# Another hand-made order for the first group of the last layer of an attention, soft-MoE and Mish kernel

## The chip, the cores and the metric

The kernel runs on one core of a Trainium2 chip. The metric is device time in microseconds of one execution. Engines are called as in the profile: PE (TensorE, matmuls; PEld its weight loads), DVE (VectorE), ACT (ScalarE), POOL (GpSimd), SP (SyncE, which issues the DMAs here).

## The reference

Three layers in float32. Attention with rotary embedding over 4 x 8 heads of 576 x 64 gives x with 2304 tokens of 512. A soft mixture of 8 experts with 4 slots each replaces x by `c @ slot_out`, where c is the softmax over the 32 slots of a token. The last layer is the one at issue:

```
def _moe2_ref(x, w_in, w_out):
    h = x @ w_in                                    # 512 -> 2048
    sp = np.where(h > 20.0, h, np.log1p(np.exp(np.minimum(h, 20.0))))
    g = h * np.tanh(sp)                             # Mish
    return (g @ w_out)                              # 2048 -> 512
```

w_in and w_out come as float64 arrays: their words are turned into float32 on the chip.

## The kernel before

Since x is c (2304 x 32) times slot_out (32 x 512), the last layer first multiplies slot_out by w_in, and each token needs only a product over 32 slots. To keep float32 accuracy with the fast fp32r matmuls, operands are split into a rounded part and a difference ("h" and "l": wo_h and wo_l for w_out, gh and gl for g; ct and wst hold both parts in their rows).

The layer's work is cut into units (i, j): 256 tokens (i, nine blocks) by 256 of the 2048 inner columns (j, eight). Three blocks make a group: group 0 is units 0 to 23, j in the outer and i in the inner loop, so three units in a row share a j. I call these three a round. Per unit:

- `mish(u)` (L992): hp = wst x ct on PE (two matmuls, L997), Mish on ACT into gg (L1004), a rounded copy gh (L1006), and gl = gg - gh on DVE (L1009).
- `second(u)` (L1014): twelve matmuls of 512 columns into the output tiles o_ps (L1028). In group 0 the eight with gh come first, then the four with gl.

Ahead of each round in group 0, `inner_a(j)` makes m_wp = slot_out x w_in on PE (L974) and copies it on ACT (L975); `inner_b(j)` makes m_w on PE (L980), copies it to wst on ACT (L982) and takes the difference of its lower half on DVE (L983). The units of round j read that part of wst. m_wp, m_w and hp share two PSUM buffers.

w_out has 16 chunks of 128 rows. The first four were converted during attention; `parts_of(c)` loads one from scratch memory and splits it (wo_h on ACT, L939; wo_l on DVE, L940). The other twelve come raw (`load_out`, four buffers, L863) and are converted by `cv(c, k)`: "S" scales the two words on ACT (L871, L872), 1 to 5 are DVE steps (L874, L876, L879, L881, L883), "H" is wo_h on ACT (L885), "L" is wo_l on DVE (L887). `convert(n)` issues the next n DVE steps of the list that `stream()` yields. `second` of round j reads chunks 2j and 2j + 1.

The order is by hand: `pin` keeps each engine's instructions in program order, and every engine works its queue in that order. In the loop at the end, unit u does `mish(u)` (from unit 3 on with `convert(4)` between gh and gl), then `inner_a(j + 1)` with i = 0 or `inner_b(j + 1)` with i = 1, then the `second` of earlier units; the lag between `mish` and `second` grows from one unit to LOOK = 4 in the course of group 0:

```
        while done < u + 1 - min(LOOK, 1 + u // 4):
            second(done)
            done += 1
```

`warm(pool, tag, n)` (L553) issues n matmuls of 128 x 128 on constants whose result nobody reads; each is two passes on PE. `fetch((3, fb, 0))` loads a quarter of the converted w_in from scratch (scr_in, 1 MB).

Of the kernel before, what the change touches and what calls it, by code (L numbers as in the profile page):

```python
# [42 lines left out]
def kernel(  # L43
# [13 lines left out]
    nc = tc.nc  # L57
    NB, H, S, D = q.shape
# [44 lines left out]
    NFC = F2 // 128  # L103

    NCE = 4
# [16 lines left out]
    def fetch(key, behind=False):  # L122
        m, e, hf = key
        t = parts[key][0]
        if m == 3:
            lds = [(t.rearrange("p (c f) -> p c f", c=KDM), scr_in[e])]
        else:
            w = (w1, w2)[m - 1]
            n = w.shape[1] // 2
            lds = [(t.rearrange("p (c f) -> p c f", c=n // 128),  # L130
                    w[e, hf * n:(hf + 1) * n, :].rearrange("(c p) f -> p c f", p=128))]
            if (m, e // 4, hf) == (2, E // 4 - 1, 1):

                final.append(lds.pop())
                if len(final) == 4:
                    lds = [(o[:, c], i[:, c]) for c in range(n // 128) for o, i in final]
        for out, in_ in lds:
            ld = nc.sync.dma_start(out=out, in_=in_)
            if behind:
                tc.keep_in_program_order(ld)  # L140
# [44 lines left out]
    behind = []  # L185
# [363 lines left out]
    def warm(pool, tag, n):  # L549

        ps = pool.tile([128, 128], F32, tag=tag, name="warm")
        for _ in range(n):
            tc.keep_in_program_order(nc.tensor.matmul(ps, lhsT=ident, rhs=ident, start=True, stop=True))  # L553
# [269 lines left out]
    for eg in range(2):  # L823
        for hf in range(2):
            end = eg == 1 and hf == 1
            for fh, cc in [(fh, cc) for fh in range(2) for cc in range(2)]:
                c = 2 * hf + cc
# [30 lines left out]
    pin = tc.keep_in_program_order  # L858

    def load_out(c):  # L860

        if c < NFC:
            pin(nc.sync.dma_start(out=raws[c % 4], in_=w_out[c * 128:(c + 1) * 128, :].bitcast(U32)))  # L863

    def cv(c, k):

        lo, hi = words(raws[c % 4])
        w = ws3[c % 3]
        wb, sf = w.bitcast(U32), sg.bitcast(F32)
        if k == "S":  # L870
            pin(nc.scalar.activation(out=hi.bitcast(F32), in_=hi.bitcast(F32), func=AF.Copy, scale=2.0 ** -112))  # L871
            pin(nc.scalar.activation(out=lo.bitcast(F32), in_=lo, func=AF.Copy, scale=2.0 ** -52))  # L872
        elif k == 1:
            pin(nc.vector.tensor_scalar(out=sg, in0=hi, scalar1=0x80000000, scalar2=None, op0=ALU.bitwise_and))  # L874
        elif k == 2:
            pin(nc.vector.scalar_tensor_tensor(out=wb, in0=hi, scalar=3, in1=sg, op0=ALU.logical_shift_left,  # L876
                                               op1=ALU.bitwise_or))
        elif k == 3:
            pin(nc.vector.tensor_scalar(out=sg, in0=wb, scalar1=0xFF800000, scalar2=None, op0=ALU.bitwise_and))  # L879
        elif k == 4:  # L880
            pin(nc.vector.tensor_tensor(out=sf, in0=sf, in1=lo.bitcast(F32), op=ALU.mult))  # L881
        elif k == 5:
            pin(nc.vector.tensor_tensor(out=w, in0=w, in1=sf, op=ALU.add))  # L883
        elif k == "H":
            pin(nc.scalar.copy(wo_h[c], w))  # L885
        else:
            pin(nc.vector.tensor_tensor(out=wo_l[c], in0=w, in1=wo_h[c].bitcast(F32), op=ALU.subtract))  # L887

    so_ps = ps_m.tile([128, DM], F32, tag="m", name="so_ps")
    for eg in range(2):  # L890
        for hf in range(2):
            for cc in range(4):
                c = 4 * hf + cc
# [31 lines left out]
        take(*rooms.pop(0))  # L925
    ot = room(F32)
    obs = [ot[:, i * DM:(i + 1) * DM] for i in range(4)]
    for c in range(NCE):
        if c == 2:
            fetch((3, 0, 0), behind=True)  # L930
        pin(nc.sync.dma_start(out=wo_l[c].bitcast(F32), in_=scr_out[c]))
    for c in range(NCE, NCE + 4):
        load_out(c)
    fetch((3, 1, 0), behind=True)

    def parts_of(c):

        x = wo_l[c].bitcast(F32)
        pin(nc.scalar.copy(wo_h[c], x))  # L939
        pin(nc.vector.tensor_tensor(out=wo_l[c], in0=x, in1=wo_h[c].bitcast(F32), op=ALU.subtract))  # L940

    def stream():

        for c in range(NCE, NFC):
            yield c, 1
            yield c, 2
            if c > NCE:
                yield c - 1, "L"
            yield c, 3
            if c + 1 < NFC:  # L950
                yield c + 1, "S"
            yield c, 4
            load_out(c + 4)
            yield c, 5
            yield c, "H"
        yield NFC - 1, "L"

    steps2 = stream()
# [1 line left out]
    def convert(n):  # L960
        while n:
            x = next(steps2, None)
            if x is None:
                return
            cv(*x)
            n -= x[1] not in ("S", "H")

    def inner_a(j):

        fb, o = divmod(j * 256, 512)  # L970
        wi = parts[3, fb, 0][0].rearrange("p (c f) -> p c f", c=KDM)[:, :, o:o + 256]
        ps = ps_p.tile([128, 256], F32, tag="p", name="m_wp")
        for c in range(KDM):
            pin(nc.tensor.matmul(ps[32 * c:32 * c + 32, :], lhsT=s_t[:, c, :], rhs=wi[:, c, :], start=True, stop=True))  # L974
        pin(nc.scalar.copy(wps[j % 2], ps))  # L975

    def inner_b(j):

        ps = ps_p.tile([128, 256], F32, tag="p", name="m_w")
        pin(nc.tensor.matmul(ps, lhsT=rr, rhs=wps[j % 2], start=True, stop=True))  # L980
        dst = wst[:, j * 256:(j + 1) * 256]
        pin(nc.scalar.copy(dst, ps))  # L982
        pin(nc.vector.tensor_tensor(out=dst[64:128], in0=ps[64:128], in1=dst[64:128].bitcast(F32), op=ALU.subtract))  # L983
# [3 lines left out]
    NG = NFC // 2  # L987
    GR = 3
# [3 lines left out]
    def mish(u):  # L992
        i, j = units[u]
        hp = ps_p.tile([128, 2, 256], F32, tag="p", name="hp")
        for x in range(2):
            f = 2 * j + x
            pin(nc.tensor.matmul(hp[:, x, :], lhsT=wst[:, f * 128:(f + 1) * 128],  # L997
                                 rhs=ct[:, i * 256:(i + 1) * 256],
                                 start=True, stop=True))
        hp = hp.rearrange("p a n -> p (a n)")  # L1000
        gg = ggs[u % 3]
        gh = p6.tile([128, 512], F32R, tag="gh", name="gh", bufs=LOOK + 1)
        gl = p6.tile([128, 512], F32R, tag="gl", name="gl", bufs=LOOK + 1)
        pin(nc.scalar.activation(out=gg, in_=hp, func=AF.Mish))  # L1004

        pin((nc.scalar.copy if u < NG * GR else nc.vector.tensor_copy)(gh, gg))  # L1006
        if 2 < u < NG * GR:
            convert(4)
        pin(nc.vector.tensor_tensor(out=gl, in0=gg, in1=gh.bitcast(F32), op=ALU.subtract))  # L1009
        gs[u] = gh, gl  # L1010

# [2 lines left out]
    def second(u):  # L1014
        i, j = units[u]
        gh, gl = gs.pop(u)
        todo = [(n, x, k) for n in range(2) for x in range(2) for k in range(3)]
        if u < NG * GR:

            todo.sort(key=lambda y: y[2] == 2)  # L1020
        if j == 0:
            for n in range(2):
                ops[i, n] = ps_o.tile([128, DM], F32, tag="o", name="o_ps")
        for at, (n, x, k) in enumerate(todo):
            g_, w_ = ((gh, wo_h), (gh, wo_l), (gl, wo_h))[k]
            f = 2 * j + x
            cols = slice(x * 256 + n * 128, x * 256 + n * 128 + 128)
            pin(nc.tensor.matmul(ops[i, n], lhsT=g_[:, cols], rhs=w_[f], start=(j == 0 and (x, k) == (0, 0)),  # L1028
                                 stop=(j == NG - 1 and all(y[0] != n for y in todo[at + 1:]))))
            if j == NG - 1 and all(y[0] != n for y in todo[at + 1:]):  # L1030
                ob = obs[(2 * i + n) % 4]
                pin((nc.scalar.copy if n else nc.vector.tensor_copy)(ob, ops.pop((i, n))))  # L1032
                store(2 * i + n, ob)
# [14 lines left out]
            pos += n  # L1048

    LOOK = 4  # L1050
    inner_a(0)
    parts_of(0)
    inner_b(0)
    parts_of(1)
    done = 0
    for u in range(len(units)):
        g, j = units[u][0] // GR, units[u][1]
        i = units[u][0] % GR
        if g == 0 and i == 2 and j in (0, 2):
            fetch((3, 2 + j // 2, 0), behind=True)  # L1060
        mish(u)
        if u in (1, 2):
            parts_of(u + 1)
        if u == 2:
            cv(NCE, "S")
        if g == 0 and j + 1 < NG:
            if i == 0:
                inner_a(j + 1)
            elif i == 1:
                inner_b(j + 1)  # L1070

        while done < u + 1 - min(LOOK, 1 + u // 4):
            second(done)
            done += 1
    while done < len(units):
        second(done)
        done += 1
    ring.close()


# [48 lines left out]
```

## Time and profile before

| | us |
|---|---|
| median of 3 runs | 679.82 |
| lowest, highest | 678.02, 682.76 |
| the profiled execution | 678.98 |
| its span, first to last instruction | 677.2 |

Times in rows are microseconds from the start of the span. A timeline row gives start, duration, engine, line, operation, written tile <- read tiles, shape and count, and in brackets the engine's idle time before it and what ended that. Matmuls are pipelined: their durations overlap, and what one costs is read from the distance of the starts. Rows name many small buffers "room".

### The profile page before, as it was taken

How to read it: one execution, taken by the hardware profiler on the slowest of the kernel's cores; microseconds unless marked ns; L12 is line 12 of the kernel's file. 1: busy time of each engine (PE TensorE's matmuls, PEld its weight loads, DVE VectorE, ACT ScalarE, POOL GpSimd, SP SyncE). 2: the span in 40 equal slices, each digit the busy share in tenths (PEclk: the TensorE clock that was granted, in tenths of full speed). 3: DMA queues.
4: the chain of work that ended last, by engine and by line, in shares of the span. 5: the costliest groups of instructions: out<-in, count | busy, mean ns of one | idle time of the engine just before them, and what ended most of it. 6: DMA issues, size and time to landing. Idle time of an engine off the chain costs nothing. (4 is left out here: it accounts for less than half of the span.)

```text
span 677.2 us, 11071 instructions
## 1 busy us (share of the span) xinstructions
PE 625.3 (92%) x4006; PEld 461.1 (68%) x4006; DVE 410.7 (61%) x823; ACT 336.3 (50%) x758; POOL 217.1 (32%) x263
## 2 busy tenths in 40 slices
PE   1588999987999999999999998998999999999997
PEld 1565677665677667667677663366688888888885
DVE  6787888886687866656565433159994433343331
ACT  2566776684676656755665412168763221221221
POOL 5658868754967545425300010000000000000000
PEclk9899999999999999999999999989999999999999
DMA  9678699877786975346559479954300300030004
GB/s 263 159 193 230 177 273 267 226 212 227 195 246 211 289 187 136 99 112 185 125 172 312 179 260 367 382 212 155 121 6 0 94 1 0 1 94 0 1 0 94
DMA packets 59607, 109.43 MB, mean 162 GB/s; under 512 B 12832, under 2 KB 25248, under 8 KB 59040
## 3 DMA queue, kind: packets, MB, share of 16 engines
q1 hardware_dynamic: 59552, 108.72, 53.8%
q8 instruction: 32, 0.52, 0.3%
q14 instruction: 23, 0.19, 0.1%
HBM read 70.25 MB, written 9.96 MB: 118 GB/s over the span
## 5 line engine op out<-in xcount | busy, mean ns | idle before, releaser
L361 DVE TENSOR_REDUCE nmax<-s 128x1 f32<-128x576 f32 x144 | 108.0, 753 | 61.0 <-PE s L335 38.3
L367 ACT ACTIVATE P<-s,nmax 128x576 f32<-128x576 f32 x144 | 107.3, 745 | 41.0 <-DVE nmax L361 29.0
L1028 PE MATMUL o_ps<-wo_h,gh 128*128 128x512 f32 x288 | 115.4, 401 | 0.0
L1028 PE MATMUL o_ps<-wo_l,gh 128*128 128x512 f32 x288 | 113.5, 394 | 0.0
L1004 ACT ACTIVATE room<-hp 128x512 f32<-128x512 f32 x72 | 43.1, 598 | 117.4 <-PE hp L997 113.0
L1028 PE MATMUL o_ps<-wo_h,gl 128*128 128x512 f32 x288 | 100.4, 389 | 0.0
L333 PE MATMUL s<-qk_st 128*128 128x288 f32 x256 | 84.9, 346 | 11.9 <-ACT P L367 6.5
L374 PE MATMUL t<-cs,P 128*128 128x128 f32 x512 | 78.6, 281 | 4.8 <-ACT P L367 2.7
L410 ACT COPY PT<-t 128x512 f32<-128x512 f32 x92 | 53.6, 587 | 48.4 <-PE t L374 47.5
L429 PE MATMUL m_av<-PT,w 128*64 128x320 f32 (+1 forms) x384 | 73.3, 421 | 3.6 <-DVE PT L413 2.1
L374 PEld LDWEIGHTS t<-cs,P 128*128 128x128 f32 x512 | 59.3, 142 | 22.1 <-issue 10.9
L335 PE MATMUL s<-k_st,qk_st 128*128 128x288 f32 x256 | 73.0, 299 | 0.0
L333 PEld LDWEIGHTS s<-qk_st 128*128 128x128 f32 x256 | 49.2, 192 | 31.7 <-ACT P L367 10.7
L1006 DVE CAST gh<-room 128x512 fp32r<-128x512 f32 x48 | 20.5, 427 | 79.2 <-ACT room L1004 79.2
L1028 PEld LDWEIGHTS o_ps<-wo_h,gh 128*128 128x128 f32 x288 | 54.6, 190 | 11.8 <-issue 2.1
L231 POOL TENSOR_TENSOR w<-w,cs 128x512 f32<-128x512 f32 x34 | 44.8, 1317 | 54.6 <-PE m_k L285 47.3
L1028 PEld LDWEIGHTS o_ps<-wo_h,gl 128*128 128x128 f32 x288 | 54.1, 188 | 11.7
L1028 PEld LDWEIGHTS o_ps<-wo_l,gh 128*128 128x128 f32 x288 | 54.8, 190 | 9.3
L1009 DVE TENSOR_TENSOR gl<-room,gh 128x512 fp32r<-128x512 f32 x72 | 49.7, 690 | 16.1 <-ACT gh L1006 10.7
L335 PEld LDWEIGHTS s<-k_st,qk_st 128*128 128x128 f32 x256 | 49.6, 194 | 0.0
L228 POOL TENSOR_TENSOR w<-w,cs 128x512 f32<-128x512 f32 x34 | 45.2, 1330 | 7.9 <-DMA w<-in_k_dram 3.7
L429 PEld LDWEIGHTS m_av<-PT,w 128*64 128x64 f32 x384 | 26.5, 136 | 24.6 <-issue 9.2
(175 smaller groups left out, 1011.8 us busy)
## 6 DMA issues: line engine op xcount, KB each, us to landing
w<-in_moe_w_dram SPq DMA_DIRECT2D x28, 1024.0 KB, 7.8
w<-in_moe_w_in_dram SPq DMA_DIRECT2D x16, 512.0 KB, 6.7
qk_st<-parth SPq DMA_DIRECT2D x46, 144.0 KB, 3.3
qk_st<-partl SPq DMA_DIRECT2D x46, 144.0 KB, 3.2
room<-in_moe_w_out_dram SPq DMA_DIRECT2D x12, 512.0 KB, 3.5
w<-in_q_dram SPq DMA_DIRECT2D x16, 256.0 KB, 5.2
w<-in_k_dram SPq DMA_DIRECT2D x16, 256.0 KB, 4.5
w<-in_moe_w_dram SPq DMA_DIRECT2D x16, 256.0 KB, 5.4
```

Source lines behind the costliest of these rows:

```text
L228: eng.tensor_tensor(out=tb, in0=src, in1=sin.to_broadcast([128, n, w]), op=ALU.mult)
L231: eng.tensor_tensor(out=dst, in0=sv, in1=cv, op=ALU.mult)
L333: nc.tensor.matmul(s[:, half, 0:288], lhsT=st[:, qc:qc + 128], rhs=st[:, KC + o:KC + o + 288], start=first, stop=False)
L335: nc.tensor.matmul(s[:, half, 0:288], lhsT=st[:, qc:qc + 128], rhs=k2_st[p % 2][:, o:o + 288], start=False, stop=last)
L361: nc.vector.tensor_reduce(out=stat[p][0][:, i:i + 1], in_=s[:, :, 0:288], axis=AX.XY, op=ALU.max, negate=True)
L367: nc.scalar.activation(out=P[p, t][:, h * S:(h + 1) * S].rearrange("p (a b) -> p a b", a=2), in_=s[:, :, 0:288], func=AF.Exp, bias=stat[p] ...
L374: nc.tensor.transpose(ps[:, j, :], P[p, t][:, blk * 128:(blk + 1) * 128], ident)
L410: nc.scalar.copy(dst, src)
L429: nc.tensor.matmul(ps[o:o + 64, :], lhsT=lhsT, rhs=rhs, start=(c == 0), stop=(c == 4))
L1004: pin(nc.scalar.activation(out=gg, in_=hp, func=AF.Mish))
L1009: pin(nc.vector.tensor_tensor(out=gl, in0=gg, in1=gh.bitcast(F32), op=ALU.subtract))
L1028: pin(nc.tensor.matmul(ops[i, n], lhsT=g_[:, cols], rhs=w_[f], start=(j == 0 and (x, k) == (0, 0)), stop=(j == NG - 1 and all(y[0] != n fo ...
```

## The change

In group 0, the conversions start with unit 0 and take 3 DVE steps a unit, 4 in the first of a round; a unit's gl is no longer made in `mish` but in `rest`, which stands one unit later, ahead of that unit's conversion steps; "H" and "L" of a chunk come later in the list; the lag of `second` is one unit throughout group 0 and two afterwards. `inner_a` and `inner_b` move from i = 0 and 1 to i = 1 and 2, and stand behind the `second` of their unit. gh of unit 0 goes to DVE. Between the first steps stand 3, 6 and 5 calls of `warm` (`idle`). Among the loads, scr_in's first quarter and the first raw chunk move ahead of some of the scratch loads of w_out. No arithmetic is added but the warm-up matmuls.

```diff
+    fetch((3, 0, 0), behind=True)
     for c in range(NCE):
         if c == 2:
-            fetch((3, 0, 0), behind=True)
+            load_out(NCE)
         pin(nc.sync.dma_start(out=wo_l[c].bitcast(F32), in_=scr_out[c]))
-    for c in range(NCE, NCE + 4):
+    for c in range(NCE + 1, NCE + 4):
         load_out(c)
...
         for c in range(NCE, NFC):
             yield c, 1
+            if c > NCE:
+                yield c - 1, "H"
             yield c, 2
+            yield c, 3
             if c > NCE:
                 yield c - 1, "L"
-            yield c, 3
             if c + 1 < NFC:
                 yield c + 1, "S"
             yield c, 4
             load_out(c + 4)
             yield c, 5
-            yield c, "H"
+        yield NFC - 1, "H"
         yield NFC - 1, "L"
...
-        pin((nc.scalar.copy if u < NG * GR else nc.vector.tensor_copy)(gh, gg))
-        if 2 < u < NG * GR:
-            convert(4)
+        pin((nc.scalar.copy if 0 < u < NG * GR else nc.vector.tensor_copy)(gh, gg))
+        gs[u] = gh, gl, gg
+
+    def rest(u):
+
+        gh, gl, gg = gs[u]
         pin(nc.vector.tensor_tensor(out=gl, in0=gg, in1=gh.bitcast(F32), op=ALU.subtract))
         gs[u] = gh, gl
...
+    def idle(n):
+
+        warm(ps_o, "o", n)
+
     inner_a(0)
     parts_of(0)
+    idle(3)
     inner_b(0)
     parts_of(1)
-    done = 0
-    for u in range(len(units)):
-        g, j = units[u][0] // GR, units[u][1]
-        i = units[u][0] % GR
+    cv(NCE, "S")
+    idle(6)
+    for u in range(len(units) + 2):
+
+        lag = 1 if u < NG * GR else 2
+        if u < len(units):
+            g, j = units[u][0] // GR, units[u][1]
+            i = units[u][0] % GR
+            mish(u)
+            if u == 0:
+                convert(3)
+                idle(5)
+            else:
+                if u in (1, 2):
+                    parts_of(u + 1)
+                if g == 0 or u == NG * GR:
+                    rest(u - 1)
+                    convert(3 + (i == 0))
+                if g:
+                    rest(u)
+        else:
+            g = None
+        if u >= lag and u != NG * GR:
+            second(u - lag)
         if g == 0 and i == 2 and j in (0, 2):
             fetch((3, 2 + j // 2, 0), behind=True)
-        mish(u)
-        if u in (1, 2):
-            parts_of(u + 1)
-        if u == 2:
-            cv(NCE, "S")
         if g == 0 and j + 1 < NG:
-            if i == 0:
+            if i == 1:
                 inner_a(j + 1)
-            elif i == 1:
+            elif i == 2:
                 inner_b(j + 1)
-
-        while done < u + 1 - min(LOOK, 1 + u // 4):
-            second(done)
-            done += 1
-    while done < len(units):
-        second(done)
-        done += 1
```

PE's order around an `inner_b` in group 0. Before, at unit 7 (m_w is for round 3, whose first unit is 9; the twelve o_ps are `second(5)`, of which five stand here, then hp of units 8 and 9):

```order
L980 MATMUL m_w<-room,cs 128x256 [waits Activation_49]
L1028 MATMUL o_ps<-wo_h_4890,gh 128x512
...
L1028 MATMUL o_ps<-wo_h_4890,gl 128x512 [waits DVE_49]
L1028 MATMUL o_ps<-wo_h_4891,gl 128x512
L1028 MATMUL o_ps<-wo_h_4890,gl 128x512
L1028 MATMUL o_ps<-wo_h_4891,gl 128x512
L997 MATMUL hp<-ct,wst 128x256 [waits Activation_49]
L997 MATMUL hp<-ct,wst 128x256
L997 MATMUL hp<-ct,wst 128x256 [waits DVE_49,Activation_49]
```

After, the same in unit 5 (m_w for round 2, hp of unit 6, which is round 2's first):

```order
L1034 MATMUL o_ps<-wo_h_4890,gl 128x512 [waits DVE_49]
L1034 MATMUL o_ps<-wo_h_4891,gl 128x512
L1034 MATMUL o_ps<-wo_h_4890,gl 128x512
L1034 MATMUL o_ps<-wo_h_4891,gl 128x512
L983 MATMUL m_w<-room,cs 128x256 [waits Activation_49]
L1000 MATMUL hp<-ct,wst 128x256 [waits DVE_49]
L1000 MATMUL hp<-ct,wst 128x256
L1034 MATMUL o_ps<-wo_h_4890,gh 128x512
```

The `second` that stood between m_w and the hp that reads its wst now stands ahead of m_w.

DVE's order at the start of the layer. Before (wo_l_4904 to wo_l_4907 are chunks 0 to 3, the rooms are the steps of chunk 4; two gl stand in one row):

```order
L940 TENSOR_TENSOR wo_l_4905<-wo_l_4905,wo_h_4889 128x512
L1009 TENSOR_TENSOR gl<-room,gh 128x512 x2
L940 TENSOR_TENSOR wo_l_4906<-wo_l_4906,wo_h_4890 128x512
L983 TENSOR_TENSOR wst<-m_w,wst 64x256
L1009 TENSOR_TENSOR gl<-room,gh 128x512
L940 TENSOR_TENSOR wo_l_4907<-wo_l_4907,wo_h_4891 128x512
L874 TENSOR_SCALAR room<-room 128x512
```

After:

```order
L941 TENSOR_TENSOR wo_l_4905<-wo_l_4905,wo_h_4889 128x512
L1009 CAST gh<-room 128x512
L874 TENSOR_SCALAR room<-room 128x512
L876 SCALAR_TENSOR_TENSOR room<-room 128x512
L879 TENSOR_SCALAR room<-room 128x512
L941 TENSOR_TENSOR wo_l_4906<-wo_l_4906,wo_h_4890 128x512
L1015 TENSOR_TENSOR gl<-room,gh 128x512
L881 TENSOR_TENSOR room<-room 128x512
L883 TENSOR_TENSOR room<-room 128x512
L874 TENSOR_SCALAR room<-room 128x512
L941 TENSOR_TENSOR wo_l_4907<-wo_l_4907,wo_h_4891 128x512
L1015 TENSOR_TENSOR gl<-room,gh 128x512
```

gl of units 0 and 1 now stand behind wo_l of chunks 2 and 3, and three steps of chunk 4 stand ahead of both.

## Rows read from the trace of the kernel before

**Rows 1.** The page: busy time by engine, and the group of gh copies on DVE.
```profile
PE 625.3 (92%) x4006; PEld 461.1 (68%) x4006; DVE 410.7 (61%) x823; ACT 336.3 (50%) x758; POOL 217.1 (32%) x263
...
L1006 DVE CAST gh<-room 128x512 fp32r<-128x512 f32 x48 | 20.5, 427 | 79.2 <-ACT room L1004 79.2
```

**Rows 2.** Windows: length, busy PE, PEld, DVE, ACT, POOL (instructions), PEclk, DMA, GB/s.
```profile
436.40:439.90 3.50, 2.46 (x20) 1.45 (x18) 0.50 (x3) 1.26 (x3) 0.00 (x0) 1.00 1.02 408
439.90:446.80 6.90, 5.89 (x21) 3.99 (x21) 4.09 (x7) 4.38 (x9) 0.00 (x0) 0.51 1.03 421
...
451.20:509.60 58.40, 54.15 (x279) 41.76 (x278) 53.44 (x95) 44.17 (x83) 0.00 (x0) 1.00 0.26 91
509.60:672.60 163.00, 163.00 (x763) 135.75 (x761) 63.05 (x110) 36.59 (x63) 0.00 (x0) 1.00 0.10 26
```

**Rows 3.** Timeline of PE, units 17 to 21.
```profile
496.44 0.40 PE L997 MATMUL hp<-ct,wst 128*128 128x256 f32 x2
...
503.17 0.40 PE L997 MATMUL hp<-ct,wst 128*128 128x256 f32 x2
503.40 0.59 PE L980 MATMUL m_w<-room,cs 128*128 128x256 f32 x2
...
504.06 0.39 PE L1028 MATMUL o_ps<-wo_l,gh 128*128 128x512 f32 x1
...
506.60 0.40 PE L997 MATMUL hp<-ct,wst 128*128 128x256 f32 x2
...
509.58 0.40 PE L997 MATMUL hp<-ct,wst 128*128 128x256 f32 x2
```

**Rows 4.** Windows: one round in the middle of group 0, columns as in rows 2.
```profile
477.60:487.00 9.40, 7.72 (x42) 5.86 (x41) 9.02 (x17) 7.47 (x15) 0.00 (x0) 1.00 0.32 112
```

**Rows 5.** Timeline of PE at the layer's start: m_wp, m_w, hp(0), later hp(3).
```profile
438.15 0.64 PE L974 MATMUL m_wp<-w,s_t 128*32 128x256 f32 x8 [0.48 <-DMA w<-scr_in]
439.27 0.70 PE L980 MATMUL m_w<-room,cs 128*128 128x256 f32 x2 [0.48 <-ACT room L975]
440.97 0.79 PE L997 MATMUL hp<-ct,wst 128*128 128x256 f32 x2 [1.01 <-DVE wst L983]
...
451.27 0.40 PE L997 MATMUL hp<-ct,wst 128*128 128x256 f32 x2
```

**Rows 6.** Timeline of ACT and DVE between that m_w and hp(0).
```profile
440.00 0.37 ACT L982 CAST wst<-m_w 128x256 fp32r<-128x256 f32 x1 [0.27 <-PE m_w L980]
...
440.49 0.43 DVE L983 TENSOR_TENSOR wst<-m_w,wst 64x256 fp32r<-64x256 f32 x1
```

**Rows 7.** Timeline of SP: the first scratch loads of w_out.
```profile
429.26 1.20 SPq L931 DMA_DIRECT2D wo_l<-scr_out  x2
```

**Rows 8.** DMA issues from 429.0 to 429.9: count, KB each, median us to landing.
```profile
wo_l<-scr_out SPq DMA_DIRECT2D x1, 256.0 KB, 5.3
```

**Rows 9.** Timeline of PE: eight warm-up calls in an earlier stretch.
```profile
391.53 2.05 PE L553 MATMUL warm<-cs 128*128 128x128 f32 x16
```

**Rows 10.** Timeline of ACT, units 2 and 3.
```profile
449.34 0.62 ACT L1006 CAST gh<-room 128x512 fp32r<-128x512 f32 x1
449.86 0.61 ACT L939 CAST wo_h<-wo_l 128x512 fp32r<-128x512 f32 x1
450.38 0.69 ACT L871 ACTIVATE room<-room 128x512 f32<-128x512 f32 x1
450.97 0.66 ACT L872 ACTIVATE room<-room 128x512 f32<-128x512 uint32 x1
451.70 0.60 ACT L1004 ACTIVATE room<-hp 128x512 f32<-128x512 f32 x1
452.33 0.62 ACT L1006 CAST gh<-room 128x512 fp32r<-128x512 f32 x1
```

**Rows 11.** Timeline of DVE, unit 2: wo_l of chunk 3 and the next.
```profile
450.60 0.68 DVE L940 TENSOR_TENSOR wo_l<-wo_l,wo_h 128x512 fp32r<-128x512 f32 x1
451.20 0.42 DVE L874 TENSOR_SCALAR room<-room 128x512 uint32<-128x512 uint32 x1
```

## The prediction

> **What bounds the kernel now.** I read the page first: PE is busy for 625.3 of the 677.2 us span [rows 1], so the question in any stretch is whether PE waits there, and for what. The change touches only the last layer (Mish and the second product), so I cut that layer into stretches. The columns to compare are the times in a stretch that PE, DVE and ACT were busy, and the granted clock, PEclk [rows 2]. From 509.6 us to the end PE is busy 163.00 of 163.00 us: nothing can be won there, and nothing is lost unless units come late. From 451.2 to 509.6, the first group, PE is busy 54.15 of 58.40 us while DVE is busy 53.44. And from 439.9 to 446.8 PE runs at 0.51 of its clock.
>
> The PE timeline late in the group gives the prices of its work at full clock [rows 3]. A unit without extras takes 509.58 - 506.60 = 2.98 us: an hp of 503.40 - 503.17 = 0.23 and a `second` of twelve matmuls of about 0.23, together 2.75. A round of three units with one `inner_a` and one `inner_b` takes 506.60 - 496.44 = 10.16. In it m_w costs 504.06 - 503.40 - 0.23 = 0.43, which leaves 10.16 - 3 x 2.98 - 0.43 = 0.79 for m_wp.
>
> What DVE does to this shows in a round somewhat earlier [rows 4]: in 9.40 us DVE is busy 9.02 and PE only 7.72. Such rounds are shorter than 10.16 because the growing lag (LOOK) leaves one `second` out; without a wait the round would be about 10.16 - 2.75 = 7.4. So there DVE, with 12 conversion steps a round, is the bound. Over the group, from the hp of unit 3 (451.27, [rows 5]) to that of unit 21 (509.58), 58.3 us pass; the work is 18 hp, 15 `second` and 6 pairs of m_wp and m_w, or 6 x 10.16 - 3 x 2.75 = 52.7 us. PE waits 5.6 us. This is the first thing the change can win.
>
> **The rounds after the change.** There are 72 conversion steps, as before, now 3 a unit from unit 0 on and 4 in the first unit of a round: 10 a round, the last in unit 21, whose own `second` comes a unit later. DVE then has 3 differences gl, 10 steps and one wst difference, 14 instructions where [rows 4] has 17 for 9.02 us: about 7.4 us a round, well inside it. The differences gl are ahead of the steps, and a unit's gl is wanted only by the ninth matmul of its `second`. So I count DVE's 5.6 us as gone.
>
> What is late next is wst. PE's order, shown with the change, has it: before, a whole `second` and an hp lie between an m_w and the hp of the next round; now that hp is the very next instruction after m_w. PE cannot start it until ACT has copied m_w and DVE has taken its difference. Behind the waiting hp stands everything else of PE, and Mish, gh and gl of the unit wait for it. The trace shows this chain once, at the start of the layer: m_w starts at 439.27, hp at 440.97 [rows 5]. In it ACT begins at 440.00, 0.73 after m_w, and takes 0.37; DVE takes 0.43 [rows 6]. DVE's start at 440.49 came somewhat late, so I take 0.73 + 0.37 + 0.03 + 0.43 + 0.05 = 1.61 us, the 0.03 and 0.05 being estimates of the handovers out of the gaps in these rows. m_w itself costs 0.43 anyway, so each occurrence costs 1.18. The bounds are PE's own idle time there, 1.01, and the whole step as measured less m_w, 440.97 - 439.27 - 0.43 = 1.27 [rows 5]. There are seven, before units 3, 6, ... 21. It costs nothing less than this unless something could run in the gap, and PE has nothing in order to run; if ACT or DVE is in the middle of a conversion step, up to 0.69 is added.
>
> A round is therefore 10.16 - 0.43 + 1.61 = 11.34, and the six from unit 3 to unit 21 take 68.0 us, with 18 `second`s. Before, 58.3 with 15; with three more, 58.3 + 3 x 2.75 = 66.6. **Sum of the rounds: +1.4 us.** What DVE gives back, the wst wait more than takes.
>
> **The start.** I walk it in times of the profile of before. m_wp starts at 438.15 as before: the load of w (scr_in) moved to the front of the queue can save at most the 0.48 us of idle time shown there [rows 5], and m_wp needs s_t as well; I take 0. The load is 1 MB, 2.6 us at the 408 GB/s of [rows 2], and the two wo_l loads that it is moved past land that much later. The first was issued at 429.26 [rows 7] and landed after 5.3 us [rows 8], so it would land at about 437.2 now; ACT wants it only after m_wp, past 439: hidden. Raw chunk 4 moves ahead of two wo_l loads, which gain about as much as that costs them and are wanted later still.
>
> A warm-up pass takes 2.05 / 16 = 0.13 us, two to a call [rows 9]. idle(3) reaches 0.2 us past the time when m_w could start: m_w at 439.45. wst would be ready 1.61 later, at 441.06, but idle(6) holds PE until 439.45 + 0.43 + 1.5 = 441.4: hp(0) at 441.4, against 440.97. idle(5) brings hp(1) to 442.9. `second(0)` starts once gh(0) is there: ACT copies m_w (from 440.2), makes wo_h of chunk 1, and now scales chunk 4 ahead of Mish(0) (two instructions, about 0.6 each [rows 10]), so Mish(0) starts at 442.1 and ends at 442.7; the copy gh(0), now on DVE, takes 0.43 [rows 1] and ends at 443.15. So `second(0)` starts at 443.2, and its eight matmuls with gh end at 445.0.
>
> Then it needs gl(0), and this difference stands on DVE behind wo_l of chunk 2, which needs wo_h of chunk 2, which ACT does after Mish(1) and gh(1). Prices: hp to Mish 451.70 - 451.27 = 0.43, Mish to gh 0.63, gh to the next 0.52, wo_h 0.61 with its end [rows 10]; wo_l 0.60 to the next, and the same shape again for gl, 0.68 [rows 11]. 442.9 + 0.43 + 0.63 + 0.52 + 0.61 + 0.60 + 0.68 = 446.4. PE waits 1.4 us. Four matmuls and m_wp later, hp(2) is at 446.4 + 0.92 + 0.79 = 448.1, and unit 2 repeats the pattern with chunk 3: gl(1) is there 3.5 us after hp(2), at 451.6, while PE has got through hp and eight matmuls by 450.2: another 1.4. Then four matmuls, m_w at 452.5, and the first wst wait: hp(3) at 454.15. Before, it was at 451.27 with the same two `second`s done. **Sum of the start: +2.9 us.** This has the full clock in it; at the clock of before it would be more (below).
>
> **The rest.** In the groups behind, the lag is 2 units instead of 4. gl of a unit is made about 2.3 us after its hp (0.43 + 0.63 + 0.43 + 0.68 and handovers), and is wanted two units, 6 us, later: nothing. At the seam (unit 24) gl(23) is queued on DVE behind the copy of an output tile and gh(24): PE could wait some tenths; I take 0.3, an estimate: Mish(24) some 0.6 behind an output copy on ACT, 0.43 for gh and 0.68 for gl end about 2.6 us after the hp, and PE wants gl at 2.3. gh(0) on DVE: in the walk.
>
> The sum: 2.9 + 1.4 + 0.3 = +4.6 us on the profiled execution's 678.98 us, 683.6 us. That execution lies 0.8 below the median of the three runs, 679.82; I leave the forecast at 683.6, which is 0.6% above that median. A measurement of this kernel tells about 1% from no change, so this should come out as no change, on the slow side.
>
> **A rule of the Trainium skill on the clock.** The profile shows the clock at 0.51 from 439.9 on, after 3.50 us in which PE was busy 2.46 [rows 2]. The page "TensorE: Matmul & The Clock Gate" (Part 1: The HAM clock gate) says that the throttled state is the default, that idleness brings it back and sustained activity releases it. By that rule the fourteen warm-up calls, which fill the gaps around m_w and hp, keep the clock up, and the sum stays at 683.6. By the row, PE was far from idle before the clock fell, so it may fall again; the second rival below prices that.
>
> **The rivals.**
> 1. *PE never waits for wst or gl* (ACT and DVE, relieved, deliver in time). For it: DVE has 4 us of air in a round. Against it: the wait is a chain of handovers, not a queue, and the order leaves no matmul to cover it. Start: `second(0)` at 443.2, m_wp, hp, `second(1)`, m_w: hp(3) at 443.2 + 2.75 + 0.79 + 0.23 + 2.75 + 0.43 = 450.15, 1.1 earlier than before; rounds 6 x 10.16 = 61.0 against 66.6, 5.6 less. Together -6.7: 672.3 us, faster by 1%. Chance 0.08.
> 2. *The clock falls as before.* Price: the 22 passes of idle(6) and idle(5) take 22 x 0.13 = 2.8 us more at half clock, and Mish and all behind it come later by that; the slow matmuls of `second(0)` lie in the wait for gl. 686.4 us. For it: the fall at 439.9 [rows 2]. Against it: PE is fuller ahead of it now. It decides if the clock is low when hp(0) is reached. Chance 0.2; half of it is over 1% slower.
> 3. *The conversions get in the way of wst*: ACT or DVE is in a step when m_w lands, in every round. 7 x 0.69 = 4.8 on top: 688.4, slower by 1.3%. Against it: DVE has 4 us of air. Chance 0.08.
>
> **How the numbers follow.** Forecast 683.6 with chance 0.64; its own range, from 1.01 to 1.27 a wst wait (-1.2, +0.6) and start waits of 0.4 to 2 us each (-2, +1.2), is 680.4 to 685.4. Faster by over 1% (under 673): most of the first rival, 0.07. Slower by over 1% (over 686.6): half of the second, the third, a tail of the forecast, 0.21. The rest, 0.72, within 1%. The range that leaves out two in ten: 677 to 687.5; its lower end stands for a shorter wst chain together with a start that does not wait for gl.
>
> **What would show it.** Right: PE rows "hp <- DVE wst" six or seven times, about 1.2 us each, and no "hp <- ACT" or "m_w <- ACT" waits in the group; "o_ps <- DVE gl" twice at the start, over 1 us each; DVE at some 70% of the group instead of 92%; rounds of 11.3 us; PE without gaps from unit 25 on; hp(3) near 454. Wrong: rounds of 10.2 us; a clock of 0.5 beyond 440 would speak for the second rival; DVE without air for the third.

## The result and the profile after

| | before | after |
|---|---|---|
| median of 6 runs | 680.52 us | 685.67 us |
| lowest, highest | 678.02, 682.76 | 684.97, 687.75 |
| the profiled execution | 678.98 us | 684.97 us |
| its span | 677.2 us | 683.2 us |

The ratio after to before is 1.0078, 95% interval 1.0052 to 1.0104: slower by 0.8%. That is clear of noise, and under the 1% up to which the prediction speaks of no change, though the interval reaches a little beyond it.

The windows of after, cut as in [rows 2] (length, then busy PE, PEld, DVE, ACT, POOL with instructions, PEclk, DMA, GB/s):

```profile
437.70:441.20 3.50, 3.04 (x27) 2.33 (x26) 0.59 (x3) 1.26 (x3) 0.00 (x0) 1.00 1.04 402
441.20:448.10 6.90, 5.82 (x38) 4.82 (x37) 5.48 (x11) 5.39 (x10) 0.00 (x0) 1.00 0.70 281
...
455.44:523.50 68.06, 62.52 (x313) 47.18 (x313) 47.70 (x85) 42.97 (x78) 0.00 (x0) 1.00 0.21 70
523.50:678.60 155.10, 155.10 (x726) 129.07 (x726) 63.70 (x112) 36.97 (x63) 0.00 (x0) 1.00 0.10 27
```

The clock is full where it was at 0.51 before. In the group DVE is busy 47.70 of 68.06 us (70%) instead of 53.44 of 58.40 (92%), and yet PE idles. For what, PE's waits in the first group tell (in total, times, longest):

```profile
PE hp L1000 <- DVE wst L986: 6.5, 7, 0.9
PE o_ps L1034 <- DVE gl L1015: 2.3, 2, 1.4
PE m_wp L977 <- DVE s_t L911: 0.4, 1, 0.4
```

Before, the waits in the rounds were for ACT (copies of m_wp and buffers of hp; the first of the four lies ahead of unit 0, 0.5 us long):

```profile
PE m_w L980 <- ACT room L975: 3.6, 4, 1.5
PE hp L997 <- ACT room L1004: 1.1, 3, 0.7
```

They are gone, and two others stand in their place. PE's timeline of after shows where; it answers to [rows 5] and [rows 3]:

```profile
439.44 0.64 PE L977 MATMUL m_wp<-w,s_t 128*32 128x256 f32 x8 [0.38 <-DVE s_t L911]
...
440.79 0.60 PE L983 MATMUL m_w<-room,cs 128*128 128x256 f32 x2
...
442.48 0.48 PE L1000 MATMUL hp<-ct,wst 128*128 128x256 f32 x2
...
447.50 1.20 PE L1034 MATMUL o_ps<-wo_h,gl 128*128 128x512 f32 x4 [0.95 <-DVE gl L1015]
...
452.89 1.19 PE L1034 MATMUL o_ps<-wo_h,gl 128*128 128x512 f32 x4 [1.35 <-DVE gl L1015]
453.92 0.59 PE L983 MATMUL m_w<-room,cs 128*128 128x256 f32 x2
455.44 0.50 PE L1000 MATMUL hp<-ct,wst 128*128 128x256 f32 x2 [0.92 <-DVE wst L986]
...
465.28 0.59 PE L983 MATMUL m_w<-room,cs 128*128 128x256 f32 x2
466.79 0.51 PE L1000 MATMUL hp<-ct,wst 128*128 128x256 f32 x2 [0.92 <-DVE wst L986]
```

m_w to hp takes 455.44 - 453.92 = 1.52 us with nothing between, and a round 466.79 - 455.44 = 11.35. The idle time in brackets is shorter than the cost, since m_w's modelled end lies late; the cost is the round less the 10.16 of [rows 3], 1.19 us. ACT and DVE between m_w and hp, and ahead of the second wait for gl:

```profile
444.98 0.62 ACT L1009 CAST gh<-room 128x512 fp32r<-128x512 f32 x1
...
450.90 0.62 ACT L940 CAST wo_h<-wo_l 128x512 fp32r<-128x512 f32 x1
...
454.55 0.37 ACT L985 CAST wst<-m_w 128x256 fp32r<-128x256 f32 x1 [2.52 <-PE m_w L983]
```

```profile
451.55 0.69 DVE L941 TENSOR_TENSOR wo_l<-wo_l,wo_h 128x512 fp32r<-128x512 f32 x1 [2.25 <-ACT wo_h L940]
452.16 0.68 DVE L1015 TENSOR_TENSOR gl<-room,gh 128x512 fp32r<-128x512 f32 x1
...
454.96 0.43 DVE L986 TENSOR_TENSOR wst<-m_w,wst 64x256 fp32r<-64x256 f32 x1 [0.45 <-ACT wst L985]
```

ACT had been idle for 2.52 us when m_w came and DVE for 0.45: neither was busy with something else. The chain is made of handovers. And DVE sat idle for 2.25 us with gl(1) behind wo_l in its queue; its own inputs, gg and gh of unit 1, had been there since 445.60 (gh on ACT at 444.98, 0.62 long), 6 us earlier.

How to compare profiles here: ahead of the first m_wp the change touches only the order of some loads, which are issued from 429 us on. Yet m_wp starts at 438.15 in the profile of before, at 439.44 after, and between 436.73 and 440.02 in the twelve profiles of this study, one of each kernel. The shift is older than the loads: the last run of 96 matmuls ahead of the layer starts at 425.42 before and at 426.81 after. So below I give, beside the ratio of the timed runs, the layer's length within a profile, from the start of the first m_wp to the end of the last o_ps, and its part up to the hp of unit 3. Before: 234.45 and 13.12. After: 239.18 and 16.00. Kernels that have the same order from hp(3) on agree there within 0.05 us (after, e2 and e3: 223.18 to 223.23; e1 and e4: 216.79 and 216.80), so that tenths can be read in that column as long as the clock does not fall.

### The profile page after: what moved, and what is told of

Same layout as the page of the kernel before. It is cut to its first block, busy times and chain, and to the rows that moved or that the text cites. A ratio compares the mean times of both kernels' runs of the same rounds, so it can differ in the third digit from the quotient of the medians.

```text
span 683.2 us, 11115 instructions
## 1 busy us (share of the span) xinstructions
PE 629.7 (92%) x4034; PEld 463.2 (68%) x4034; DVE 408.0 (60%) x824; ACT 337.2 (49%) x757; POOL 216.9 (32%) x263
## 4 chain that ended last, share of the span: by engine, by line
PE 76%; DMA 9%; DVE 6%; ACT 3%; POOL 2%; issue 1%; SPq 1%; ACTq 0%; DVEq 0%; POOLq 0%
PE o_ps L1034 29%; PE m_av L429 13%; PE t L374 7%; PE s L333 5%; PE s L335 4%; DMA w<-in_moe_w_in_dram 3%; PE hp L1000 3%; PE so_ps L896 2%; PE s L353 2%; DMA w<-in_moe_w_dram 2%; PE m_lg L455 1%; DVE nmax L361 1%; PE warm L553 1%; ACT P L367 1%; PE tk L388 1%
## 5 line engine op out<-in xcount | busy, mean ns | idle before, releaser
L1034 PE MATMUL o_ps<-wo_h,gh 128*128 128x512 f32 x288 | 113.1, 393 | 0.1
L333 PE MATMUL s<-qk_st 128*128 128x288 f32 x256 | 86.0, 351 | 11.9 <-ACT P L367 6.0
L374 PEld LDWEIGHTS t<-cs,P 128*128 128x128 f32 x512 | 59.9, 143 | 22.1 <-issue 10.2
L333 PEld LDWEIGHTS s<-qk_st 128*128 128x128 f32 x256 | 50.1, 196 | 32.0 <-ACT P L367 10.4
```

Source lines behind the costliest of these rows:

```text
L333: nc.tensor.matmul(s[:, half, 0:288], lhsT=st[:, qc:qc + 128], rhs=st[:, KC + o:KC + o + 288], start=first, stop=False)
L374: nc.tensor.transpose(ps[:, j, :], P[p, t][:, blk * 128:(blk + 1) * 128], ident)
```

## The experiments

Theory: the change costs seven waits for wst and two for gl, and wins back what PE waited for while DVE was its bound. The rivals are told with each run.

| kernel | ratio to before | 95% interval | layer, us | to hp(3) | from there |
|---|---|---|---|---|---|
| before | 1 | | 234.45 | 13.12 | 221.33 |
| after | 1.0078 | 1.0052 to 1.0104 | 239.18 | 16.00 | 223.18 |
| e1, inner ahead of second | 0.9959 | 0.9935 to 0.9982 | 231.59 | 14.80 | 216.79 |
| e2, gl ahead of wo_l | 1.0016 | 0.9995 to 1.0037 | 237.22 | 14.03 | 223.19 |
| e3, no warm-up calls | 1.0092 | 1.0061 to 1.0124 | 240.63 | 17.40 | 223.23 |
| e4, e1 and e2 | 0.9927 | 0.9901 to 0.9953 | 230.16 | 13.36 | 216.80 |
| e5, before, inner late | 1.0164 | 1.0128 to 1.0199 | 246.33 | 14.71 | 231.62 |
| e6, before, warm-up calls | 1.0006 | 0.9982 to 1.0029 | 234.91 | 11.97 | 222.94 |
| e7, e4 and wst ahead of steps | 0.9896 | 0.9859 to 0.9932 | 228.22 | 11.69 | 216.53 |
| e8, e4 with the old pace | 0.9930 | 0.9906 to 0.9954 | 229.88 | 11.66 | 218.22 |
| e9, before, constant lag | 0.9893 | 0.9867 to 0.9920 | 227.92 | 12.11 | 215.81 |
| e10, e7 with the old pace | 0.9939 | 0.9918 to 0.9960 | 230.25 | 11.64 | 218.61 |

**e1: the wst waits undone.** From the kernel after:

```diff
+        if g == 0 and j + 1 < NG:
+            if i == 1:
+                inner_a(j + 1)
+            elif i == 2:
+                inner_b(j + 1)
         if u >= lag and u != NG * GR:
             second(u - lag)
...
-        if g == 0 and j + 1 < NG:
-            if i == 1:
-                inner_a(j + 1)
-            elif i == 2:
-                inner_b(j + 1)
```

> The changed kernel with inner_a and inner_b ahead of the second of their unit, so that twelve matmuls lie between m_w and the hp that reads its wst; ACT's and DVE's order is unchanged. Theory (seven wst waits of about 1.18 us are the cost of the change): the waits 'hp <- DVE wst' vanish but for the first, rounds take 10.2 us instead of 11.35, the time falls by 7 x 1.18 = 8 us to about 677.5, ratio to before 0.995 (0.992 to 0.998). The two waits for gl at the start stay. Rival (the lag of one unit, or ACT behind the conversions, is the true limit, and the wst wait only stands where another wait would be): the waits move to 'o_ps <- gl' or 'hp <- ACT', rounds stay above 11, ratio 1.005 to 1.008.

Measured: 0.9959, and the layer is 7.6 us shorter than after. PE's waits in the first group of e1:

```profile
PE o_ps L1034 <- DVE gl L1015: 1.5, 2, 0.9
PE hp L1000 <- DVE wst L986: 0.9, 1, 0.9
```

Of the seven waits one is left, that of unit 3; from hp(3) on the layer is 223.18 - 216.79 = 6.4 us shorter, which is six waits of 1.07 each (a round now takes 10.3 us, so 0.1 of the 1.19 remains). The other 1.2 us came ahead of hp(3), where the two waits for gl shrank from 2.3 to 1.5 us in all. The order on ACT and DVE is the same as in the kernel after, so the place of m_w on PE alone costs this. The theory holds, and moving twelve matmuls behind m_w makes the change a gain.

**e2: the gl waits undone.**

```diff
-                if u in (1, 2):
-                    parts_of(u + 1)
                 if g == 0 or u == NG * GR:
                     rest(u - 1)
+                    if u in (1, 2):
+                        parts_of(u + 1)
                     convert(3 + (i == 0))
```

> The changed kernel with gl of units 0 and 1 ahead of wo_l of chunks 2 and 3 on DVE (and of wo_h on ACT). Theory (gl behind wo_l costs two waits, 2.3 us of PE idle time in the profile): both waits shrink below 0.5 us, the time falls by 2 to 2.8 us to about 683.2, ratio 1.004 (1.001 to 1.006). Rival (the first units are bound by the chain hp, Mish, gh anyway): ratio stays at 1.008. The wst waits stay.

Measured: 1.0016, the layer 1.96 us shorter, all of it ahead of hp(3). The waits for gl are gone:

```profile
PE hp L1000 <- DVE wst L986: 7.1, 7, 1.5
PE m_wp L977 <- DVE s_t L911: 0.4, 1, 0.4
```

But the longest wait for wst grew from 0.9 to 1.5, at unit 3, where wst stands behind wo_l of chunk 3 and three steps on DVE. That is why 1.96 came and not the 2.6 that the two waits had cost (1.1 and 1.5 by the starts of the matmuls). The medians of the timed runs differ by more, 685.67 against 681.48; no trace here shows where the other 2 us lie.

**e3: no warm-up calls.**

```diff
-        warm(ps_o, "o", n)
+        return
```

> The changed kernel with the fourteen warm-up calls left out. Theory (they hold the clock up and delay hp(0) by 0.4 us): the granted clock falls to 0.5 about 440 us in, for some 3 to 7 us; the slow stretch costs 1 to 3 us, part of it hidden in the waits for gl: 686.5 to 688, ratio 1.010 (1.007 to 1.013). Rival (the clock falls or stays whatever these calls do, and they only delay): clock as in the changed kernel, 0.4 us less, ratio 1.007.

Measured: 1.0092, the layer 1.45 us longer, all ahead of hp(3). The granted clock fell again (windows of e3):

```profile
440.00:444.10 4.10, 2.08 (x14) 0.99 (x14) 1.81 (x3) 3.10 (x7) 0.00 (x0) 1.00 1.04 412
444.10:451.00 6.90, 6.10 (x20) 4.00 (x20) 4.81 (x9) 3.07 (x6) 0.00 (x0) 0.51 0.61 227
```

So the calls hold the clock up, as the theory has it: without them PE was busy 2.08 of 4.10 us and then ran at half clock for 6.9 us. Part of that lies in the waits for gl. It is not one profile alone that says so: in all four kernels without the calls (before, e3, e5, e9) the clock is at half for 3.4 to 6.9 us at the start of the layer, in none of the eight with them.

**e4: both edits.** The diffs of e1 and e2 together.

> inner_a and inner_b ahead of second, and gl ahead of wo_l: the first two edits together. Theory: the two costs are independent and add: 685.7 - 8 - 2.5 = 675.2, ratio 0.992 (0.989 to 0.996), PE idle in the first group below 2 us. Rival (with both gone the next wait, for gl of unit 0 behind the three steps of chunk 4 or for the m_w copy, takes their place): ratio 0.996 to 1.0.

Measured: 0.9927, the layer 9.0 us shorter than after; e1 and e2 alone gave 7.6 and 2.0. The costs add up but for half a microsecond. What is left in PE's waits:

```profile
PE hp L1000 <- DVE wst L986: 1.5, 1, 1.5
PE m_wp L977 <- DVE s_t L911: 0.4, 1, 0.4
```

**e5: the late place of inner_a and inner_b alone, in the kernel before.**

```diff
+        while done < u + 1 - min(LOOK, 1 + u // 4):
+            second(done)
+            done += 1
         if g == 0 and j + 1 < NG:
-            if i == 0:
+            if i == 1:
                 inner_a(j + 1)
-            elif i == 1:
+            elif i == 2:
                 inner_b(j + 1)
-
-        while done < u + 1 - min(LOOK, 1 + u // 4):
-            second(done)
-            done += 1
```

> The kernel before with one part of the change alone: inner_a and inner_b at i = 1 and 2, behind the second of their unit (all else, the growing lag and the pace too, as before). Theory (this placing costs 1.18 us in each round in which PE is the bound, and less where PE waits for DVE anyway): waits 'hp <- DVE wst' appear in all seven rounds; two rounds at full pace cost the whole 1.2, the DVE-bound ones part of it, since the hp that waits also holds back Mish and gl, which DVE's queue has ahead of its conversions: 3 to 7 us slower, ratio 1.004 to 1.010. Rival (in before the wait is covered, as the backlog of seconds and DVE's bound leave air): ratio 0.998 to 1.002.

Measured: 1.0164; the layer is 11.9 us longer than before, well beyond the 3 to 7 that the theory gave. The waits are there, the longest far longer than in after, and the clock fell twice more (waits, two windows and three rows of e5):

```profile
PE hp L997 <- DVE wst L983: 11.6, 8, 2.9
```

```profile
465.50:468.90 3.40, 3.40 (x10) 2.63 (x9) 3.24 (x7) 2.08 (x4) 0.00 (x0) 0.51 0.25 76
...
475.70:482.50 6.80, 5.33 (x14) 4.27 (x15) 5.76 (x11) 3.34 (x7) 0.00 (x0) 0.50 0.36 127
```

```profile
473.55 0.70 PE L980 MATMUL m_w<-room,cs 128*128 128x256 f32 x2
...
476.30 0.36 ACT L982 CAST wst<-m_w 128x256 fp32r<-128x256 f32 x1
...
477.17 0.79 PE L997 MATMUL hp<-ct,wst 128*128 128x256 f32 x2 [2.92 <-DVE wst L983]
```

The sign is the theory's and not the rival's. The size is not: in a group where ACT and DVE are full, the chain also stands in their queues. In the longest wait, 2.9 us, ACT began the copy of an m_w of 473.55 only at 476.30, behind four instructions of its own (gh, "S" and "H"). The two stretches at half clock, 10.2 us in all, can hold at most 5.1 of the 11.9 us, an estimate by the granted clock of 0.5. How much is queue and how much clock was not taken apart.

**e6: the warm-up calls alone, in the kernel before.**

```diff
+    def idle(n):
+        warm(ps_o, "o", n)
...
     parts_of(0)
+    idle(3)
     inner_b(0)
     parts_of(1)
+    idle(6)
...
         mish(u)
+        if u == 0:
+            idle(5)
```

> The kernel before with the fourteen warm-up calls alone, at the same places (three ahead of inner_b(0), six ahead of unit 0, five behind its mish). Theory (they keep the clock up at the price of some 1.5 us in which PE is held back): granted clock 1.0 from 440 us on; second(0) and the m_wp and m_w around it run at full speed, which wins about 2 us, and hp(0) and hp(1) come 0.4 and 0.3 us later: ratio 0.998 (0.995 to 1.001). Rival (the chain over ACT and DVE sets the start, the slow clock is hidden): ratio 1.000 to 1.003 with the clock at 1.0.

Measured: 1.0006: no difference. Up to hp(3) the layer is 1.15 us shorter and the clock is full there, but later it fell where it had not before (windows of e6):

```profile
438.00:449.90 11.90, 11.84 (x78) 9.61 (x79) 5.47 (x10) 7.87 (x16) 0.00 (x0) 1.00 0.77 311
449.90:482.20 32.30, 28.06 (x148) 20.86 (x147) 29.79 (x54) 25.98 (x50) 0.00 (x0) 1.00 0.37 130
482.20:485.60 3.40, 3.40 (x10) 2.64 (x9) 3.24 (x7) 1.43 (x3) 0.00 (x0) 0.50 0.44 154
```

That stretch cost the gain again, 1.6 us (222.94 against 221.33 from hp(3) on): up to it and behind it the two profiles have the same rounds, and the same waits for ACT. The last 4 us ahead of the fall in e6, and the same units in the kernel before:

```profile
478.20:482.20 4.00, 2.32 (x17) 1.36 (x17) 3.87 (x8) 3.83 (x9) 0.00 (x0) 0.99 0.38 131
```

```profile
479.50:483.50 4.00, 2.32 (x18) 1.40 (x16) 3.88 (x8) 3.83 (x9) 0.00 (x0) 1.00 0.37 131
483.50:487.00 3.50, 3.50 (x18) 2.89 (x18) 3.34 (x7) 1.77 (x4) 0.00 (x0) 1.00 0.44 150
```

PE was busy for the same 2.32 of 4.00 us, and there the clock stayed at 1.00. So this profile does not show that the calls brought the later fall, nor whether the other executions lost their gain in the same way. It shows that a clock held at one place can be lost at a later one.

**e7: wst ahead of the steps.** From e4, inner_a and inner_b right behind `rest`:

```diff
                     rest(u - 1)
+                    if g == 0 and j + 1 < NG:
+                        if i == 1:
+                            inner_a(j + 1)
+                        elif i == 2:
+                            inner_b(j + 1)
                     if u in (1, 2):
                         parts_of(u + 1)
                     convert(3 + (i == 0))
```

> The version with both edits, and in addition inner_a and inner_b ahead of the conversion steps (and of wo_l) of their unit, right behind gl of the unit before, so that the wst difference does not stand behind wo_l of chunk 3 and three steps in unit 2. Theory (the 1.5 us that hp of unit 3 still waits for wst there is DVE's order alone): that wait goes, no other of over 0.5 us comes, 1 to 1.5 us less than with both edits: ratio 0.990 (0.987 to 0.994). Rival (DVE, which now waits in every round for m_w and its copy before it goes on, falls behind with the conversions): waits 'o_ps <- DVE wo_l' or 'gl' in late rounds, ratio 0.993 to 0.998.

Measured: 0.9896; the layer is 1.9 us shorter than in e4, 1.7 of it ahead of hp(3). The edit moves m_w's copy on ACT as well, but in e4 that copy had ended at 449.46 and the difference began only at 451.08, with DVE busy throughout: that wait was DVE's order. PE waits for nothing in the group that its own rows show.

**e8: the old pace in e4.**

```diff
-                convert(3)
...
-                    convert(3 + (i == 0))
+                    if u > 2:
+                        convert(4)
```

> The version with both edits, but with the pace of before: four conversion steps a unit from unit 3 on and none ahead of it. Theory (DVE was the bound before only in rounds that the growing lag had cut short; a round of three seconds takes PE 10.16 us and DVE with 12 steps 9.4): the even pace as such is worth nothing once the lag is constant: ratio as with both edits within 0.002, 0.991 to 0.995; in the first units it may win some tenths, since gl no longer stands behind steps. Rival (the even pace from unit 0 on is what removes PE's waits for DVE): PE waits for DVE reappear in units 3 to 20, 2 to 5 us, ratio 0.996 to 1.000.

Measured: 0.9930 against e4's 0.9927: in sum the even pace is worth nothing, as the theory has it. The layer's parts show that this sum has two terms: without conversion steps in the first units hp(3) comes 1.70 us earlier, and the rest takes 1.42 longer (rounds of 10.4 us instead of 10.3).

**e9: the constant lag alone, in the kernel before.** One line:

```diff
-        while done < u + 1 - min(LOOK, 1 + u // 4):
+        while done < u + 1 - (1 if u < NG * GR else 2):
```

> The kernel before with the lag of second alone changed: one unit in group 0, two afterwards (pace, places of inner_a and inner_b, place of gl, loads as before, no warm-up calls). Theory (before, PE waited some 5.6 us in group 0 because the growing lag takes a second out of three rounds and leaves them to DVE's 9.4 us; with the lag constant each round has 10.16 us of PE work to cover them): most of the 5.6 us go, the start of the layer stays as in before: 3.5 to 6 us less, ratio 0.993 (0.990 to 0.996). Rival (the pace of the conversions, or gl behind four steps, is what made PE wait): PE waits 'o_ps <- DVE gl' or 'wo_l' in group 0 take the place of the others, ratio 0.998 to 1.003.

Measured: 0.9893 (0.9867 to 0.9920), beyond the expectation and with e7 the best of all. From hp(3) on the layer is 221.33 - 215.81 = 5.5 us shorter. PE's waits in the first group and a window of e9:

```profile
PE hp L997 <- DVE wst L983: 1.0, 1, 1.0
PE m_w L980 <- ACT room L975: 0.5, 1, 0.5
PE m_wp L974 <- DVE s_t L911: 0.4, 1, 0.4
```

```profile
451.20:509.60 58.40, 58.40 (x297) 46.64 (x296) 51.73 (x91) 42.07 (x79) 0.00 (x0) 1.00 0.26 91
```

All three waits lie ahead of unit 0. In the stretch in which PE was busy 54.15 of 58.40 us before, it is now busy throughout, with the same 12 conversion steps a round and DVE at 51.73. The remaining 1.0 us came ahead of hp(3), where the clock was at half for 3.4 us in this profile and for 6.8 in that of before; that part may differ from run to run.

**e10: the old pace in e7.** The diff of e8.

> The best version so far (both edits, and inner_a and inner_b ahead of the conversion steps) with the pace of before, four steps a unit from unit 3 on. Theory (the pace is indifferent while a round of DVE's, 9.4 us and up to 1.5 of waiting for m_w's copy, fits 10.16): 0.990, within 0.003 of the version with the even pace. Rival (12 steps and the wait for the copy no longer fit into a round, so that DVE falls behind from round to round): PE waits for gl or wo_l in rounds 2 to 6, ratio 0.993 to 0.998.

Measured: 0.9939; the expectation failed, and the rival's range holds it. The layer is 2.0 us longer than e7's. PE's weight loads show why, seven waits where e7 has two of 0.6 us in total:

```profile
PEld o_ps L1034 <- DVE gl L1015: 3.6, 7, 1.3
```

Matmuls and their loads stand so close here that the wait shows in the loads' rows and hardly in the matmuls'. From hp(3) on the old pace costs 2.1 us here (218.61 - 216.53) and cost 1.4 in e4's order. What differs is the part ahead of hp(3): in e4's order the old pace won 1.70 us there, and here 0.05, since wst stands ahead of the steps already. A reason for the late gl that fits, not tested apart: with wst ahead of the steps DVE waits in every round for m_w's copy, and then 12 steps a round make gl late.

## Why the prediction was right, point by point

The forecast was 683.6 us, 0.6% above the median; measured was 685.67, 0.8% above the median of six runs, just above the forecast's own range (680.4 to 685.4) and inside the wide one (677 to 687.5).

- *The wst wait, 1.18 us seven times.* Right: it costs 11.35 - 10.16 = 1.19 a round. By its parts the chain was a little shorter than forecast, 1.52 instead of 1.61, and the hp behind it a little longer. e1 takes six of the seven away, and from hp(3) on the layer falls by 6.4 us.
- *The start, +2.9 us.* Right: hp(3) is 16.00 us after the first m_wp, forecast 454.15 - 438.15 = 16.0. gl(0) held PE for 447.50 - 446.17 - 0.23 = 1.1 us (forecast 1.4), gl(1) for 452.89 - 451.15 - 0.23 = 1.5 (forecast 1.4). e2 confirms the cause.
- *The rounds, +1.4 us.* Right in the sum: the 18 units from hp(3) to hp(21) took 68.0 us as forecast (455.44 to 523.43). Not right in the reason: the step that gave the credit for DVE's 5.6 us to the pace of the conversions. e9 shows that the constant lag gives it back, 5.5 us, without touching the pace. With the lag constant the even pace is worth 1.4 to 2.1 us from hp(3) on (e8, e10), in orders in which inner_b stands nearer to its reader than in e9; the even pace with the growing lag was not run. That this term came out is in part luck: the change held the lag constant as well. DVE's round was forecast at 7.4 us and took 47.70 / 6 = 7.95. The prediction had the reason in hand where it said that the lag cuts these rounds short, and did not draw it: at full length a round lasts 10.16 us on PE and 9.4 on DVE, so DVE need not be the bound of a full round, and in e9, with 12 steps a round, it is not.
- *The seam, +0.3, and the rest, nothing.* From hp(21) to the end 155.2 us; 51 units and a second at [rows 3]'s prices are 154.7. The wait at the seam shows only in PE's weight loads, once, 0.3 us.
- *The sum, +4.6 us.* The layer is 4.73 us longer. The profiled execution is 1.4 above the forecast because its layer began 1.29 us later, a shift that was there before the first load that the change moves. Added to the median of six runs, 680.52, the same +4.6 would give 685.1.
- *The clock.* The second rival fell: clock 1.00 from 437.7 on in the profiled execution. The Trainium skill's page "TensorE: Matmul & The Clock Gate" (Part 1: The HAM clock gate) says that activity releases the throttle; after and e3 agree with it as far as the warm-up calls go. The same part of the Trainium skill's page ties the throttled state to an idle PE; here the measurement decides, and in e3 PE was busy half of the time ahead of the fall. The other five executions of after have a mean granted clock of 0.989 to 0.994 against 0.998 in the profiled one, so the clock fell more often there; where, no trace shows.
- *The first rival* (no waits) and *the third* (conversions in the way of wst) did not come: ACT and DVE were idle when m_w landed. The third is what e5 shows where ACT and DVE are full.

## What to carry to other kernels

When an order by hand moves a small product and its copies, look at what stands between it and its first reader on the engine that is the bound: a chain over three engines costs 1.5 us here each time that the reader is next in the queue, of which 0.43 is the product itself, and about 0.1 a round when one unit's work lies between (e4: rounds of 10.3 us instead of 10.16). An engine that is busy 9.02 of 9.40 us, as DVE in [rows 4], is not thereby the bound; ask first whether the bound engine was given less work in that stretch than it could have had, since a lag that grows does just that. And try the single parts of a larger reordering alone: one line of this change gave more than the whole of it took, and the rest turned it around.

## What the runs showed of the hardware that was not expected

The clock fell to half after stretches in which PE was far from idle: busy 2.08 of 4.10 us in e3, and 2.32 of 4.00 in e6 in the middle of the group. The same 2.32 of 4.00, in the same units, left it at 1.00 in the kernel before: one profile that keeps its clock does not tell that the next will. Warm-up calls held it where they stood, in eight profiles of eight; in e6 it fell later all the same. And with the same instructions ahead of it, the last layer began as early as 436.73 us (e8) and as late as 440.02 us (e3) after the start of the span. These 3.3 us are more than the six runs of after differ among themselves (2.8 us): differences of one or two microseconds between two profiles are better read within the layer than off the span.
